# Attention maxima and scores on four tiles of 64 by 64 of the matmul array, in a transformer block kernel

## The chip, the cores and the metric

The kernel runs on one core of one Trainium2 chip, as one program. The metric is the device time of one execution in microseconds, lower is better. The core has five engines that run side by side: TensorE (PE in the profile, PEld for its weight loads), VectorE (DVE), ScalarE (ACT), GpSimd (POOL) and SyncE (SP, which here only starts DMAs). Matmul results land in PSUM, 128 partitions by eight banks of 512 fp32 values.

## The reference

One pre-norm transformer block over x of 2048 tokens by 640: sliding-window attention, then a gated feed-forward part. All inputs are fp32.

```python
S, D, H, Dh, W, F = 2048, 640, 32, 20, 256, 1536
# attention on layernorm(x): q, k, v of 32 heads with 20 features each
scores = einsum("bhqd,bhkd->bhqk", q, k) * Dh ** -0.5
mask = (iq - ik >= 0) & (iq - ik < 256)
p = softmax(where(mask, scores, -1e9))
h = x + (einsum("bhqk,bhkd->bhqd", p, v) -> (B, S, D)) @ wo
# feed-forward on layernorm(h)
h2 = h + (gelu(hn @ w_gate) * (hn @ w_up)) @ w_down
```

## The kernel before

**Blocks and windows.** The tokens are cut in 16 blocks of 128. A block of queries sees three blocks of keys: the block two before it (the oldest), the one before it, and itself (the newest); block 0 sees one and block 1 two. Of the oldest block a query in row r sees the keys in columns c > r, of the newest those with c <= r, so together the two halves of the mask make one full block.

**Numbers in two parts.** fp32 values are split into a high and a low fp16 part. For q and k the 20 features become 60 rows (high with high, high with low, low with high), so one matmul of 60 rows gives the product of one head. Heads of one parity lie on partitions 0 to 59, those of the other on 64 to 123.

**Two passes over the scores.** For each block and each unit of four heads of one parity (eight units a block) the kernel makes two passes:

- `maxima` (L1041): matmuls with queries as rows out and keys as columns (60 rows in, 128 by 128 out), into a set of three PSUM banks, one bank for each key block. `max_out` (L1135) lets VectorE copy the visible part of the oldest block over the hidden part of the newest (`copy_predicated`), then takes the maximum over the remaining two banks. When a block has all maxima, `max_rows` and `max_transpose` split them into two fp16 rows, and a DMA puts these beside the queries (rows 60 and 61).
- `scores` (L1053): the transposed product with keys as rows out and queries as columns, now with 62 rows in, so that the maximum is subtracted in the matmul. `score_out` (L1184) lets ScalarE take the exponential of all three banks, and GpSimd sets the hidden parts to zero (`affine_select`).

`value_lane` (L1198) multiplies the exponentials with the values, four heads beside each other on 32 columns of the array each, in fp32; the sums come from a column of ones.

**Two units beside each other.** There are two sets of PSUM banks (`SETS`, 0 to 2 and 3 to 5). `row_need` (L1089) picks two units of different parity, mostly one of maxima and one of scores, and `row_lane` (L1123) issues their matmuls in turn. Since one uses the lower and the other the upper 64 rows of the array, two matmuls can run at once. I call the run of matmuls of such a couple of units a stretch: 12 matmuls for each unit with three key blocks, 24 in all.

**The order of the work.** The program is written out by a planner in the kernel file itself. `Clock` and `Engine.cost` (L248) give every instruction a cost, keep a time for each engine, and the loop at the end takes the first lane of work that can start at the planned time. The order on each engine is thus fixed when the program is built, and a changed cost can change the order of all engines' instructions, and of the DMAs issued from the SP and ACT queues. The matmul part of the cost knows three layouts of the array: "full", "row" (up to 64 rows in) and "col" (up to 32 columns out); a change between them costs `SWITCH` = 0.095 us, a matmul 1/2400 us a column, at least 0.027, plus 0.0027, and one that starts beside another 0.004.

Between the stretches PE does dense work: q, k and v projections of later blocks, the output projection, and parts of the feed-forward part. After the last block (from some 560 us on) only the feed-forward part is left.

Of the kernel before, what the change touches and what calls it, by code (L numbers as in the profile page):

```python
# [23 lines left out]
P = 128  # L24
# [31 lines left out]
class Clock:  # L56
# [6 lines left out]
    def __init__(self, nc):  # L63
        self.nc = nc
        self.t = dict.fromkeys(self.NOW, 0.0)
        self.wr, self.rd, self.rings = {}, {}, {}
        self.warm, self.win, self.use = False, 0, 0.0
        self.mode, self.half = "full", 0
        self.moved, self.used = dict.fromkeys(self.NOW, 0.0), []
        self.lands = deque([0.0] * 8, maxlen=8)  # L70
        self.port = {"vector": deque(maxlen=6), "gpsimd": deque(maxlen=6)}
        for e in self.NOW:
            setattr(self, e, Engine(self, e))
# [74 lines left out]
    def warmth(self, cost, rows):  # L148

        k = int(self.t["tensor"] / self.WINDOW)  # L150
        if k > self.win:
            u = self.use / self.WINDOW if k == self.win + 1 else 0.0
            self.warm = u > 0.4 if self.warm else u > 0.75
            self.win, self.use = k, 0.0
        if not self.warm:
            cost *= 2
        self.use += cost * rows / 128
        return cost
# [19 lines left out]
    def pipe(self, at, cost):  # L178

        gaps = []  # L180
        for a, z in self.used:
            if at < a:
                gaps.append((at, min(a, at + cost)))
                cost -= gaps[-1][1] - at
                if cost <= 0:
                    break
            at = max(at, z)
        if cost > 0:
            gaps.append((at, at + cost))
        self.used = sorted(self.used[-150:] + gaps)  # L190
        return gaps[-1][1]
# [31 lines left out]
class Engine:  # L223
# [24 lines left out]
    def cost(self, op, out, ins):  # L248
        n = out.free_size()
        if op.startswith("dma_start"):  # L250
            size = n * out.partition_size() * mybir.dt.size(out.dtype)
            if op.endswith("transpose"):
                return size / 130e3
            return size / (320e3 if mybir.dt.size(out.dtype) == 4 else 150e3)
        half = mybir.dt.size(out.dtype) == 2 and ins and mybir.dt.size(ins[0].dtype) == 2
        if self.name == "tensor":
            n = ins[1].free_size()
            if op == "transpose":
                n = ins[0].partition_size()
            passes = 1 if mybir.dt.size(ins[0].dtype) == 2 else 2 if op == "transpose" else 4  # L260
            rows, cols = ins[0].partition_size(), out.partition_size()
            mode = "full" if op == "transpose" else "row" if rows <= 64 else "col"
            mode = "full" if mode == "col" and cols > 32 else mode
            k = self.clock
            switch, k.mode = SWITCH * (k.mode != mode), mode
            at = (ins[0] if mode == "row" else out).start_partition()
            beside, k.half = mode != "full" and at > k.half and not switch, at
            if beside:
                return 0.004
            return switch + k.warmth(max(n * passes / 2400, 0.027), rows) + 0.0027  # L270
        if self.name == "vector":
            m = max([n] + [i.free_size() for i in ins])
            if op in ("copy_predicated", "tensor_reduce"):
                return (0.12 if ins[-1].space == PSUM else 0.065) + 0.00106 * m
            if op == "tensor_copy" and half or op == "tensor_scalar" and m > 320:
                return (0.065 if half else 0.185) + 0.00053 * m
            return 0.065 + 0.00106 * m + 0.06 * (op == "scalar_tensor_tensor" and len(ins) == 3)
        if self.name == "scalar":
            return 0.00084 * n + (0.05 if op == "copy" or len(ins) == 1 else
                                  0.14 if ins[0].space == PSUM else 0.18)  # L280
        if self.name == "gpsimd":
            if op == "memset":
                return 0.06 + 0.0008 * n
            return 0.46 if n == 1 else 0.06 + (0.00105 if op == "affine_select" else 0.00203) * n
        raise NotImplementedError(self.name)
# [3 lines left out]
def block_kernel(ctx: ExitStack, tc: tile.TileContext, x, wqkv, wo, wg, wu, wd, out):  # L289
    nc = Clock(tc.nc)  # L290
# [9 lines left out]
    ps8 = psum.tile([P, 8 * 512], F32, name="ps8")  # L300
# [471 lines left out]
    def key(rs, pr, kb):  # L772

        return kT[rs, kb // 2 % (RK // 2), pr, kb % 2 * P:kb % 2 * P + P]
# [23 lines left out]
        pos["ones"] = 1  # L798

    nc.vector.memset(ps8[:, MM * 512:], 0.0)  # L800

    esc = const.tile([P, 1], F32, name="esc")
    hsc = const.tile([P, 1], F32, name="hsc")
# [23 lines left out]
    class Block:  # L827
        ready = wide = False
        maxima = halves = v = 0
        h, turned, normed = None, False, False  # L830
# [12 lines left out]
    at = lambda n, shape, dt, bufs=2: nc.tile(att, shape, dt, n, bufs)  # L843
# [186 lines left out]
    def window(j):  # L1030
        return list(range(max(0, j - 2), j + 1))

    def heads(u):

        return u % 2, range(4 * (u // 2), 4 * (u // 2) + 4)

    def set_view(banks):
        b = nc.box(banks[0])[1][2] // BANK
        return ps8[:, b * 512:(b + 3) * 512].rearrange("p (t c k) -> p t c k", t=3, c=4)

    def maxima(j, u, banks):  # L1041
        b = B[j]
        par, prs = heads(u)
        rs = slice(64 * par, 64 * par + 60)
        v = set_view(banks)
        ks = window(j)
        for c, pr in enumerate(prs):
            for i, kb in enumerate(ks, 3 - len(ks)):
                yield v[:, i, c, :], b.c.qT[rs, pr, b.cols], key(rs, pr, kb)
        tasks.append(max_out(j, u, banks))  # L1050
        pos["max"] += 1

    def scores(j, u, banks):  # L1053
        b = B[j]
        par, prs = heads(u)
        rs = slice(64 * par, 64 * par + 62)
        v = set_view(banks)
        ks = window(j)
        b.pt[u] = at("pt", [P, 3, 4, P], F32, 3)
        pos["units"] += 1  # L1060
        for i, kb in enumerate(ks, 3 - len(ks)):
            for c, pr in enumerate(prs):
                yield v[:, i, c, :], key(rs, pr, kb), b.c.qT[rs, pr, b.cols]
        tasks.append(score_out(j, u, banks, b.pt[u]))
        pos["score"] += 1

# [54 lines left out]
    row = []  # L1121

    def row_lane():  # L1123
        while True:
            yield ("tensor",), row_need
            gens = []
            for s, (f, x) in enumerate(row):
                (maxq if f is maxima else scoreq).remove(x)
                gens.append(f(*x, row_set(s)))
            for ops in zip_longest(*gens):  # L1130
                for op in ops:
                    if op:
                        nc.tensor.matmul(*op, start=True, stop=True)

    def max_out(j, u, banks):  # L1135
        b = B[j]
        par, prs = heads(u)
        mx = b.mx[:, 16 * par + prs[0]:16 * par + prs[0] + 4]
        n = len(window(j))
        v = set_view(banks)  # L1140
        yield on("vector", v[:, 3 - n:])
        if n == 3:
            nc.vector.copy_predicated(v[:, 2], late4, v[:, 0])
            w = v[:, 1:]
        else:
            nc.vector.tensor_tensor(v[:, 2], v[:, 2], mask4, op=ALU.add)
            w = v[:, 3 - n:]
        yield on("vector", w)
        nc.vector.tensor_reduce(mx, w.rearrange("p t c k -> p c t k"), axis=AX.XY, op=ALU.max)
        free_set(banks)  # L1150
        b.maxima += 4
        if b.maxima == H:
            tps.append(max_rows(j))
# [30 lines left out]
    def score_out(j, u, banks, pt):  # L1184
        n = len(window(j))
        v = set_view(banks)[:, 3 - n:]
        yield on("scalar", v)
        nc.scalar.activation(pt[:, 3 - n:], v, AF.Exp, scale=esc)
        free_set(banks)
        yield on("gpsimd", pt[:, 3 - n])  # L1190
        if n == 3:
            nc.gpsimd.affine_select(pt[:, 0], pt[:, 0], pattern=[[0, 4], [-1, P]],
                                    compare_op=ALU.is_ge, fill=0.0, base=-1, channel_multiplier=1)
        nc.gpsimd.affine_select(pt[:, 2], pt[:, 2], pattern=[[0, 4], [1, P]],
                                compare_op=ALU.is_ge, fill=0.0, base=0, channel_multiplier=-1)
        valq.append((j, u))
# [632 lines left out]
    rows = Lane(row_lane())  # L1829
    values = Lane(value_lane())  # L1830
    now = 0.0
# [84 lines left out]
```

## Time and profile before

| | |
|---|---|
| median of 3 runs | 997.33 us (992.41, 997.52, 997.33) |
| profiled execution, own time | 994.03 us |
| its span | 992.3 us |
| PE busy | 949.6 us, 11,637 matmuls recorded |
| weight loads (PEld) busy | 736.5 us |
| VectorE busy | 731.7 us |
| ScalarE busy | 472.7 us |
| GpSimd busy | 239.9 us |
| mean granted clock of PE | 0.998 |

The span is the time from the first to the last instruction of one profiled execution. Nearly all instructions carry the line L232, which is the helper that records every operation; the groups are told apart by the names of their tiles (`ps` is PSUM; `ps<-kT,qT` with 60 rows are maxima, `ps<-qT,kT` with 62 rows scores, `ps<-pt,vals` the value product) and by their shapes. One fp32 matmul of the program is recorded as two. A matmul's duration in the profile runs from its start to a modelled end and overlaps with its neighbours'; the time from start to start tells what it costs.

### The profile page before, as it was taken

To read this page: it belongs to the slowest core of one execution; us is meant where nothing else is said; L and a number is where in the kernel's file an instruction comes from. 1 tells how busy PE (TensorE), PEld (TensorE's weight loads), DVE (VectorE), ACT (ScalarE), POOL (GpSimd) and SP (SyncE) were. 2 spreads that over 40 slices of the span, in tenths; PEclk is the share of its full clock that TensorE was granted. 3 is DMA by queue.
4 is the path that set the end of the run, shared out by engine and by line. 5 is a ranking of instruction groups with operands and counts; after the bars stand their busy time and mean duration, and the time that the engine had idled before them with its cause. 6 is when DMAs were issued, how large, how long until landed. Compare 5 with 4: busy or idle time off the path is not lost.

```text
span 992.3 us, 27153 instructions
## 1 busy us (share of the span) xinstructions
PE 949.6 (96%) x11637; PEld 736.5 (74%) x11637; DVE 731.7 (74%) x1369; ACT 472.7 (48%) x703; POOL 239.9 (24%) x338
## 2 busy tenths in 40 slices
PE   6897999999999999999998998999999999999998
PEld 5676677777777777776764555888888888888886
DVE  6978697797856776766685689699787773994563
ACT  6624567646556555555578635553222131332120
POOL 3321234535435434334345200000111100000000
PEclk9999999999999999999999999999999999999999
DMA  9367477563453524233375523641325310120002
GB/s 351 97 167 198 121 177 187 115 155 79 99 145 58 134 69 123 69 106 78 98 181 130 156 69 112 187 120 45 94 55 148 79 68 1 45 71 14 1 2 106
DMA packets 108777, 106.89 MB, mean 108 GB/s; under 512 B 58992, under 2 KB 79728, under 8 KB 106736
## 3 DMA queue, kind: packets, MB, share of 16 engines
q1 hardware_dynamic: 85552, 94.40, 35.8%
q10 hardware_dynamic: 23104, 10.75, 4.1%
q8 instruction: 91, 1.49, 0.7%
q14 instruction: 30, 0.25, 0.1%
HBM read 71.11 MB, written 20.97 MB: 93 GB/s over the span
## 4 chain that ended last, share of the span: by engine, by line
PE 76%; DVE 10%; DMA 5%; ACT 5%; issue 2%; POOL 1%; ACTq 0%; SPq 0%; DVEq 0%; POOLq 0%
PE ps L232 76%; DVE mxs L232 2%; ACT pt L232 2%; DMA qk<-qks 1%; DVE ps L232 1%; DVE xt L232 1%; DVE qks L232 1%; DMA kT<-qk 1%; ACT wsl L232 1%; DVE kT L232 1%; POOL pt L232 1%; DMA ol<-spl 1%; DMA lxn<-h_dram 0%; ACTq L232 0%; DMA xh<-sph 0%
## 5 line engine op out<-in xcount | busy, mean ns | idle before, releaser
L232 ACT ACTIVATE pt<-ps,esc 128x1536 f32<-128x1536 f32 (+2 forms) x128 | 186.1, 1459 | 108.2 <-PE ps L232 97.9
L232 POOL TENSOR_SCALAR_AFFINE_SELECT pt<-pt 128x512 f32<-128x512 f32 x240 | 150.5, 650 | 234.9 <-ACT pt L232 232.8
L232 DVE TENSOR_REDUCE mxs<-ps 128x4 f32<-128x1024 f32 (+1 forms) x128 | 151.2, 1185 | 2.7
L232 PEld LDWEIGHTS <-kT 62*128 62x128 f16 (+1 forms) x1920 | 123.8, 95 | 27.5 <-issue 9.4
L232 DVE COPY_PREDICATED ps<-mask,ps 128x512 f32<-128x512 int32 x112 | 77.4, 693 | 77.3 <-PE ps L232 76.7
L232 DVE TENSOR_TENSOR gel<-gel,ps 128x512 f32<-128x512 f32 x140 | 93.8, 684 | 54.3 <-PE ps L232 50.1
L232 PEld LDWEIGHTS <-wu 128*128 128x128 f16 x1080 | 105.7, 98 | 12.2
L232 PEld LDWEIGHTS <-gu 128*128 128x128 f16 x888 | 86.2, 98 | 34.4 <-issue 1.3
L232 PE MATMUL ps<-kT,qT 60*128 60x128 f16 x1440 | 101.8, 218 | 7.3 <-DVE mxs L232 3.6
L232 PEld LDWEIGHTS <-qT 60*128 60x128 f16 x1440 | 79.6, 94 | 35.2 <-issue 34.5
L232 PE MATMUL ps<-qT,kT 62*128 62x128 f16 x1440 | 98.8, 218 | 3.5 <-ACT pt L232 3.3
L232 PE MATMUL ps<-pt,vals 128*21 128x128 f32 x2880 | 93.9, 276 | 6.7 <-POOL pt L232 3.2
L232 PEld LDWEIGHTS ps<-pt,vals 128*21 128x21 f32 x2880 | 73.7, 101 | 19.5 <-POOL pt L232 6.1
L232 DVE SCALAR_TENSOR_TENSOR ht<-ps,ffk,ht 128x320 f32<-128x320 f32 x96 | 51.8, 547 | 41.9 <-PE ps L232 41.7
L232 PEld LDWEIGHTS <-ah 128*128 128x128 f16 x448 | 43.7, 98 | 19.6 <-ACT ah L232 2.6
L232 ACT ACTIVATE gel<-gel,ffk 128x512 f32<-128x512 f32 x40 | 28.6, 719 | 49.9 <-DVE gel L232 49.8
L232 PE MATMUL ps<-wdh,ah 128*128 128x320 f16 x160 | 47.9, 299 | 2.2 <-ACT ah L232 2.2
L232 PE MATMUL ps<-xh,w0h 128*128 128x256 f16 x175 | 47.8, 273 | 2.1 <-ACT vals L232 1.1
L232 PE MATMUL ps<-w2l,xh 128*128 128x320 f16 x160 | 47.9, 299 | 1.5 <-DVE w2l L232 1.3
L232 PE MATMUL ps<-w3h,oh 128*128 128x320 f16 x160 | 47.9, 300 | 1.1 <-ACT oT L232 0.5
L232 PE MATMUL ps<-wdh,al 128*128 128x320 f16 x160 | 47.8, 299 | 1.2 <-DVE al L232 1.2
L232 PE MATMUL ps<-xh,w1h 128*128 128x256 f16 x175 | 47.8, 273 | 1.2 <-DVE qks L232 1.2
(252 smaller groups left out, 2267.9 us busy)
## 6 DMA issues: line engine op xcount, KB each, us to landing
wsl<-in_wd_dram SPq DMA_DIRECT2D x28, 320.0 KB
wsl<-in_wg_dram SPq DMA_DIRECT2D x33, 256.0 KB
qk<-qks ACTq DMA_DIRECT2D x64, 128.0 KB
wsl<-in_wu_dram SPq DMA_DIRECT2D x30, 256.0 KB
qT<-qk SPq DMA_DIRECT2D x16, 320.0 KB
kT<-qk SPq DMA_DIRECT2D x16, 320.0 KB
ht<-in_x_dram SPq DMA_DIRECT2D x16, 320.0 KB
h_dram<-ht SPq DMA_DIRECT2D x16, 320.0 KB
```

Source lines behind the costliest of these rows:

```text
L232: r = real(*args, **kw)
```

## The change

The array is used as four places of 64 rows by 64 columns. Each matmul of a maxima or scores unit becomes two, one for the lower and one for the upper 64 rows of the output. A unit has 24 matmuls instead of 12, and a stretch 48.

For maxima with three key blocks, `quarters` leaves out the half of the oldest block that the upper 64 queries don't see and the half of the newest that the lower 64 don't see. For each head there are then three steps of two matmuls: oldest (lower queries) with middle (upper), middle (lower) with newest (upper), and last two matmuls of 64 columns, the first half of the newest for the lower and the second half of the oldest for the upper queries. With fewer key blocks, and for scores, all is computed; the scores now go head by head as the maxima do. The tiles that VectorE, ScalarE and GpSimd then work on are the same as before. Two memsets at the start set the parts of PSUM that no maxima matmul has written to zero.

The planner gets a fourth layout, "quad", in which each of four places has a time of its own at which it is free.

```diff
@@ Engine.cost
             mode = "full" if mode == "col" and cols > 32 else mode
+            mode = "quad" if mode == "row" and cols == 64 else mode
             k = self.clock
             switch, k.mode = SWITCH * (k.mode != mode), mode
             at = (ins[0] if mode == "row" else out).start_partition()
-            beside, k.half = mode != "full" and at > k.half and not switch, at
+            if mode == "quad":
+                at = 2 * at + ins[0].start_partition()
+            if mode == "quad":
+                now = k.t["tensor"]
+                if switch or now > k.quad_end + 1e-6:
+                    k.quad, k.last = {}, now + switch - 0.004
+                k.last = max(k.last + 0.004, k.quad.get(at, 0.0))
+                k.quad[at] = k.last + max(n / 2400, 0.027) + 0.0027
+                more = max(0.001, max(k.quad.values()) - now)
+                more = switch + k.warmth(more - switch, rows)
+                k.quad_end = now + more
+                return more
+            beside, k.half = mode in ("row", "col") and at > k.half and not switch, at
@@ start
     nc.vector.memset(ps8[:, MM * 512:], 0.0)
+    for i in range(2):
+        nc.vector.memset(ps8[64:P, 3 * i * 512:3 * i * 512 + 512], 0.0)
@@ maxima
+    def quarters(n):
+        full = [((i, 0, P), (i, 0, P)) for i in range(3 - n, 3)]
+        if n < 3:
+            return full
+        return [((0, 0, P), (1, 0, P)), ((1, 0, P), (2, 0, P)), ((2, 0, 64), (0, 64, P))]
...
         for c, pr in enumerate(prs):
-            for i, kb in enumerate(ks, 3 - len(ks)):
-                yield v[:, i, c, :], b.c.qT[rs, pr, b.cols], key(rs, pr, kb)
+            for two in quarters(len(ks)):
+                for h, (i, a, z) in enumerate(two):
+                    kb = ks[i - 3]
+                    q = slice(c0 + 64 * h, c0 + 64 * h + 64)
+                    yield (v[64 * h:64 * h + 64, i, c, a:z], b.c.qT[rs, pr, q],
+                           key(rs, pr, kb)[:, a:z])
@@ scores
-        for i, kb in enumerate(ks, 3 - len(ks)):
-            for c, pr in enumerate(prs):
-                yield v[:, i, c, :], key(rs, pr, kb), b.c.qT[rs, pr, b.cols]
+        for c, pr in enumerate(prs):
+            for two in [((i, 0, P), (i, 0, P)) for i in range(3 - len(ks), 3)]:
+                for h, (i, a, z) in enumerate(two):
+                    kb = ks[i - 3]
+                    yield (v[64 * h:64 * h + 64, i, c, a:z],
+                           key(rs, pr, kb)[:, 64 * h:64 * h + 64],
+                           b.c.qT[rs, pr, c0 + a:c0 + z])
```

More of the change, by code (lines that the diff above doesn't have):

```diff
@@ L67, in __init__ @@
         self.warm, self.win, self.use = False, 0, 0.0
-        self.mode, self.half = "full", 0
+        self.mode, self.half, self.quad, self.quad_end, self.last = "full", 0, {}, 0.0, 0.0
         self.moved, self.used = dict.fromkeys(self.NOW, 0.0), []
@@ L1046, in maxima @@
         ks = window(j)
+        c0 = b.cols.start
         for c, pr in enumerate(prs):
-            for i, kb in enumerate(ks, 3 - len(ks)):
-                yield v[:, i, c, :], b.c.qT[rs, pr, b.cols], key(rs, pr, kb)
+            for two in quarters(len(ks)):
[4 more added lines that the diff above has]
+                           key(rs, pr, kb)[:, a:z])
         tasks.append(max_out(j, u, banks))
@@ L1060, in scores @@
         pos["units"] += 1
-        for i, kb in enumerate(ks, 3 - len(ks)):
-            for c, pr in enumerate(prs):
-                yield v[:, i, c, :], key(rs, pr, kb), b.c.qT[rs, pr, b.cols]
+        c0 = b.cols.start
+        for c, pr in enumerate(prs):
[5 more added lines that the diff above has]
+                           b.c.qT[rs, pr, c0 + a:c0 + z])
         tasks.append(score_out(j, u, banks, b.pt[u]))
```

## The prediction

> **What bounds the kernel now.** I read the page's busy table first, then busy time by stage, then who waits for whom, then single rows of the timeline.
>
> ```profile
> PE 949.6 (96%) x11637; PEld 736.5 (74%) x11637; DVE 731.7 (74%) x1369; ACT 472.7 (48%) x703; POOL 239.9 (24%) x338
> PE 76%; DVE 10%; DMA 5%; ACT 5%; issue 2%; POOL 1%; ACTq 0%; SPq 0%; DVEq 0%; POOLq 0%
> ```
> ```profile
> 0.00:104.00 104.00, 86.13 (x717) 69.53 (x719) 83.68 (x208) 54.44 (x108) 26.27 (x43) 1.00 0.67 201
> 104.00:560.00 456.00, 438.90 (x7434) 327.03 (x7434) 328.44 (x563) 281.38 (x368) 193.99 (x277) 1.00 0.50 121
> 560.00:992.30 432.30, 424.55 (x3502) 339.96 (x3491) 319.55 (x598) 136.84 (x228) 19.61 (x19) 1.00 0.25 71
> ```
> ```profile
> PE ps L232 <- ACT pt L232: 3.3, 6, 1.0
> PE ps L232 <- POOL pt L232: 2.4, 5, 1.7
> PE ps L232 <- ACT oT L232: 2.2, 7, 0.6
> PE ps L232 <- DVE mxs L232: 1.5, 5, 0.6
> ```
>
> TensorE (PE) is busy 96% of the span and is 76% of the chain that ended last. The stages' first number after the length is PE's busy time: attention is done between 104 and 560 us, and there PE is busy 438.9 of 456.0 us at full clock, so 17.1 us are idle. The last fence is who PE waited for in that stage (us, times, longest); these four rows are 9.4 us. VectorE, ScalarE and GpSimd have slack there. So the change counts through PE's time in the maxima and scores, and through what the planner's new order does to those waits.
>
> ```profile
> L232 PE MATMUL ps<-kT,qT 60*128 60x128 f16 x1440 | 101.8, 218 | 7.3 <-DVE mxs L232 3.6 <-DVE lyax L232 1.2 <-DMA kT<-qk 0.9
> L232 PE MATMUL ps<-qT,kT 62*128 62x128 f16 x1440 | 98.8, 218 | 3.5 <-ACT pt L232 3.3
> L232 DVE TENSOR_REDUCE mxs<-ps x128: 681/1224/1226, 59.8 to 515.4; 128x4 f32<-128x1024 f32 x120, 128x4 f32<-128x512 f32 x8
> ```
> ```profile
> 501.34 0.23 PE L232 MATMUL ps<-kT,qT 60*128 60x128 f16 x1
> 501.34 0.23 PE L232 MATMUL ps<-qT,kT 62*128 62x128 f16 x1
> 501.41 0.22 PE L232 MATMUL ps<-kT,qT 60*128 60x128 f16 x1
> 501.41 0.22 PE L232 MATMUL ps<-qT,kT 62*128 62x128 f16 x1
> 501.46 0.22 PE L232 MATMUL ps<-kT,qT 60*128 60x128 f16 x1
> 501.47 0.22 PE L232 MATMUL ps<-qT,kT 62*128 62x128 f16 x1
> ...
> 501.96 0.22 PE L232 MATMUL ps<-kT,qT 60*128 60x128 f16 x1
> 501.97 0.22 PE L232 MATMUL ps<-qT,kT 62*128 62x128 f16 x1
> 502.11 0.31 PE L232 MATMUL ps<-pt,vals 128*21 128x128 f32 x4
> ```
>
> The forms tell maxima (60 rows) from scores (62 rows): 1440 matmuls each, for 128 groups of four heads each (128 reductions), two groups to a stretch, so about 128 stretches. One whole stretch is shown: a maxima and a score matmul start together, the next pair about 56 ns later, twelve pairs in 0.63 us, and 0.14 us after the last start the next kind of matmul begins. The length in the second column (0.22 us) is latency; the start-to-start time is the cost.
>
> **The change part by part.** The sum is made against the profiled execution: span 992.3 us, own time 994.03 us.
>
> *Twice the matmuls, four at a time.* Each unit of twelve matmuls of 128 columns becomes 24 of 64 columns out: 1440 more maxima and 1440 more scores, and as many loads. A step of the new loop is lower maxima, lower score, upper maxima, upper score. Each of the four places streams 128 columns, as each of the two did, so a step should keep the 56 ns of the rows above, and twelve steps remain twelve. Of three maxima steps for a head, one streams only 64 columns; but the score matmuls beside it stream 128, and matmuls start in program order, so the next maxima matmul waits for the score ahead of it. I cost the halved step at nothing saved wherever a score runs beside it. The nearest row for four places working at once is the value product, four column places of 32:
>
> ```profile
> 502.11 1.51 PE L232 MATMUL ps<-pt,vals 128*21 128x128 f32 x48
> L232 PE MATMUL ps<-pt,vals 128*21 128x128 f32 x2880 | 93.9, 276 | 6.7 <-POOL pt L232 3.2 <-DVE qks L232 1.8 <-ACT wsl L232 1.1
> ```
> Its 48 recorded matmuls take (1.51 - 0.27) / 47 = 26 ns each, so four need 106 ns, and together they read four different fp32 streams from the same partitions; the new maxima read two fp16 streams from each partition. Reading should not bind. The bounds of a step are 28 ns (if halved ones ran free) and 106 ns (four at the row's rate); I take 56, the rows at these very shapes, because the four starts at 502.11 fall within 0.05 us of each other (below).
>
> *Weight loads.* 64 columns instead of 128:
> ```profile
> L232 PEld LDWEIGHTS <-qT 60*128 60x128 f16 x1440 | 79.6, 94 | 35.2 <-issue 34.5
> L232 PEld LDWEIGHTS <-m 128*64 128x64 f16 x16 | 1.7, 106 | 3.0 <-issue 1.5 <-DVE m L232 0.5 <-DVE ps L232 0.4
> L232 PEld LDWEIGHTS ps<-pt,vals 128*21 128x21 f32 x2880 | 73.7, 101 | 19.5 <-POOL pt L232 6.1 <-issue 4.4 <-ACT wsl L232 1.4
> L232 PEld LDWEIGHTS ps<-ident,oT 117*128 117x128 f32 x128 | 14.3, 141 | 4.5 <-ACT oT L232 2.1 <-issue 0.4
> ```
> The only 64-column fp16 load of the trace, that of the maxima's transpose, takes 106 ns against 94 for the 128-column ones. Within a stretch a load runs under the matmuls of the step before; only the first is exposed: 12 ns x 128 stretches = +1.5 us. If that cover is gone, the four loads of a step show: an estimate from 101 ns for 21 and 141 for 128 fp32 columns is 0.37 ns a column, 24 ns for 64 columns, 96 ns for four in a row.
>
> *Four starts instead of two* at the end of each stretch: the value row has four within 0.05 us, so at most about 17 ns apart; the pairs are under 10. I take 8 ns more a stretch, +1.0 us; ends 0 and 35 ns x 128 = 4.5 us.
>
> *Maxima with nothing, or a shorter score, beside them.* Blocks with shorter windows leave such tails: four rows are single in the stretch at 120.3.
> ```profile
> 120.33 0.21 PE L232 MATMUL ps<-qT,kT 62*128 62x128 f16 x1 [0.96 <-ACT pt L232]
> 120.33 0.23 PE L232 MATMUL ps<-kT,qT 60*128 60x128 f16 x1
> 120.38 0.21 PE L232 MATMUL ps<-qT,kT 62*128 62x128 f16 x1
> 120.40 0.22 PE L232 MATMUL ps<-kT,qT 60*128 60x128 f16 x1
> ...
> 120.74 0.38 PE L232 MATMUL ps<-kT,qT 60*128 60x128 f16 x4
> ```
> There a halved step saves 28 ns. Counted along the timeline: two in each of some eight such stretches, three in two more, and four in each of two stretches of maxima alone: 30 x 28 ns = -0.8 us.
>
> *Changing the array's layout*: 0.14 us from last start to next kind, of which 0.056 is streaming. No row shows a layout of 64 by 64; I count the gap unchanged, as its nearest row is the one from these very pairs to the value product's four places; a price of 0 to 30 ns more (a third of the 0.09) would be up to +4 us.
>
> *Two memsets* of 64 x 512 go behind the one of 128 x 1024 on VectorE:
> ```profile
> 1.42 0.91 DVE L232 MEMSET ps<- 128x1024 f32 x1 [0.21 <-issue]
> 2.33 0.06 DVE L232 MEMSET am<- 128x1 f32 x1
> 3.95 0.89 DVE L232 BATCH_NORM_STATS2 lstx<-xt 128x6 f32<-128x320 f32 x2 [1.57 <-DMA xt<-in_x_dram]
> ```
> At half the columns each is about 0.46 us; 0.9 us fit into the 1.57 us in which VectorE waits for x. Behind them in the queue is the layernorm, for which PE's first transposes wait; without that wait they would cost 0.9 us. I count 0.
>
> *Instructions.* PE's list grows by 5760 of 23,274.
> ```profile
> q8 instruction: 91, 1.49, 0.7%
> ```
> That is 64 B each, so +0.37 MB, some 23 fetches more beside 106 MB of other transfers: 0.
>
> *VectorE, ScalarE, GpSimd, SP*: no instruction of theirs changes beyond the memsets; the copies, reductions and exponentials still take whole tiles. No DMA is added or moved by the diff itself.
>
> *The planner.* It costed a pair at 0.0533 + 0.0027 + 0.004 = 0.060 us, twelve pairs and a switch at 0.815 us (0.867 when the upper half comes first); it now costs twelve steps at 0.095 + 12 x 0.056 + 0.012 = 0.78. What the trace shows for a stretch is 0.63 + 0.14 = 0.77. So the plan's PE clock gets 0.04 to 0.09 us a stretch earlier, nearer the chip, and many instructions of all engines, with their DMAs on the SP and ACT queues, may change places. Its worth is bounded by the 17.1 us of idle time on the one side and as much again on the other; with neither sign argued by a row I take 0.
>
> Sum: 994.0 + 1.5 + 1.0 - 0.8 = 995.7, say 996. The profiled execution is 3.3 us under the median of the three runs, 997.33, so the forecast is no change. A measurement of this kernel tells about 0.5% (5 us) from none: its three runs lie 5 us apart.
>
> **The rivals.**
>
> *Matmuls are not supplied fast enough (slower).* The densest long runs of the trace, pairs and value products, both come to 26 to 28 ns a matmul with its load. If that is a limit of supply, a stretch of 48 needs 48 x 27 = 1.30 us, not 0.68: +0.62 x 128 = 79 us, 1075. It decides from the point where fewer than 48 - 0.68 / 0.027 = 23 matmuls stand ready when a stretch begins; with 16 ready it is 16 + 32 x 27 ns = 0.86, +23 us, 1019. For it: nothing in the trace runs longer at a faster rate. Against: the four at 502.11,
> ```profile
> 502.11 0.14 PEld L232 LDWEIGHTS ps<-pt,vals 128*21 128x21 f32 x8
> ```
> with eight loads in the same 0.05 us, so twelve instructions were ready at once. Chance 0.08. The Trainium skill, "TensorE: Matmul & The Clock Gate", Part 1, puts a floor of about 25 ns on start to start, however few columns; by it the stretch would be 1.2 us and the time an estimated 1060. The trace goes against it between places of one array, with four starts in 0.05 us.
>
> *Loads of places in the same rows wait for each other (slower).* Four in a row are the 96 ns above, so a step is 96 instead of 56: 40 x 12 x 128 = +61 us, 1057; from 14 ns a load on it shows. Against: the eight loads just shown overlap and share all 128 rows; but at 21 columns (8 ns each) they don't decide it. Chance 0.06. The Trainium skill, "TensorE: Matmul & The Clock Gate", Part 3, says that a load overlaps running matmuls only where the row group differs; upper and lower half of a unit have the same rows, so by it this case would come. The value loads here run under matmuls of their own rows, which speaks against the rule for column places.
>
> *The new order waits more (slower).* A planned stretch comes earlier and finds its set of banks not yet read: 3.3 / 6 = 0.55 us a time by the ScalarE row. Eighteen more such waits in 128 stretches are +10 us, 1006. Chance 0.14.
>
> *The new order waits less (faster).* A truer PE clock lets the planner put projection work where PE waits now; eight of the 17.1 us would give 988. Chance 0.12.
>
> *The halved step counts everywhere (faster).* If maxima could run ahead of scores, four steps x 28 ns x 112 stretches = -12.5 us, 983. For it: at 120.3 the two halves run out of step, each at its own 56 ns. Against: each start still comes after the one ahead of it in the program. Chance 0.05.
>
> **How the numbers follow.** Forecast (991 to 1001): 0.55. The range 986 to 1012 holds it, most of the two cases of order and part of the -12.5 us, together about 0.8. Outside are the stretched steps, 0.14, and the tails. Faster by over 0.5% means below 992: 0.17 from two rivals and a little of the forecast's low end, 0.20. Slower: 0.06 + 0.08 + 0.14 less the mild part, 0.26. The rest, 0.54, is no change.
>
> **What would show it.** Right: stretches of 48 matmuls with about 0.63 us from first to last start, steps of 56 ns with four starts each, 0.14 us to the next kind, PE's idle time between 104 and 560 us near 17 us. Wrong: steps of 96 to 108 ns (loads or supply, told apart by whether the first steps of a stretch are quick and only the later ones slow), or a changed list of waits at an unchanged step (the order).

## The result, and the profile after

The changed kernel takes 1011.1 us, median of three runs (1004.87, 1011.1, 1011.87), against 997.33 before: ratio 1.012, 95% interval 1.0077 to 1.0164. It is slower. The forecast was no change at 996 us; the time lies at the upper end of the range, 1012. The profiled execution took 1011.1 us with a span of 1009.4 us.

The busy table and the shares of the chain that ended last, from the page of the changed kernel, then its clock row and its instruction transfers:

```profile
PE 959.1 (95%) x14517; PEld 744.7 (74%) x14517; DVE 736.0 (73%) x1371; ACT 476.9 (47%) x705; POOL 242.5 (24%) x338
PE 78%; DVE 8%; DMA 6%; ACT 4%; issue 2%; POOL 1%; ACTq 1%; SPq 0%; DVEq 0%; POOLq 0%
...
PEclk9998999999999999998999999999999999999999
...
q8 instruction: 113, 1.85, 0.8%
```

The 2880 more matmuls are there (14,517 recorded against 11,637), and only 9.5 us more of busy time. The span grew by 17.1 us. By stage (length, then busy time and count of PE, its weight loads, VectorE, ScalarE and GpSimd, granted clock, DMA share, GB/s):

```profile
0.00:104.00 104.00, 83.46 (x771) 67.43 (x771) 81.50 (x205) 53.17 (x105) 25.73 (x42) 0.97 0.63 195
104.00:560.00 456.00, 436.73 (x9750) 326.57 (x9749) 330.12 (x565) 266.37 (x355) 182.16 (x258) 0.99 0.52 121
560.00:1009.40 449.40, 438.88 (x4000) 350.68 (x3998) 324.34 (x603) 157.36 (x245) 34.62 (x39) 1.00 0.24 71
```

PE's idle time in the middle stage is 456.0 - 436.7 = 19.3 us, 2.2 us more than before; but less of the attention work is done by 560 us: its last stretch starts at 594.5 us, before at 555.5. So the stages no longer hold the same work, and the order of the whole kernel has changed. What PE waited for over the whole span (us, times, longest):

```profile
PE ps L232 <- DVE lyaxb L232: 8.4, 2, 8.0
PE ps L232 <- DVE qks L232: 7.7, 5, 4.8
PE ps L232 <- ACT pt L232: 6.0, 8, 1.9
PE ps L232 <- ACT oT L232: 5.2, 8, 1.1
PE ps L232 <- DVE mxs L232: 2.9, 7, 0.8
...
PE ps L232 <- issue: 1.0, 1, 1.0
```

Before, the same list had

```profile
PE ps L232 <- DVE qks L232: 4.5, 6, 0.9
```

One wait is long that was not there before: 4.8 us for `qks`. (The 8.0 us for `lyaxb` are at the start of the kernel, before and after.) Now the thing that was changed, a whole stretch of 48 matmuls, in the timeline of the changed kernel (start, length, form):

```profile
502.16 0.24 PE L232 MATMUL ps<-kT,qT 60*64 60x128 f16 x1
502.17 0.24 PE L232 MATMUL ps<-qT,kT 62*64 62x128 f16 x1
502.17 0.24 PE L232 MATMUL ps<-kT,qT 60*64 60x128 f16 x1
502.17 0.24 PE L232 MATMUL ps<-qT,kT 62*64 62x128 f16 x1
502.24 0.22 PE L232 MATMUL ps<-kT,qT 60*64 60x128 f16 x1
502.25 0.22 PE L232 MATMUL ps<-qT,kT 62*64 62x128 f16 x1
502.25 0.22 PE L232 MATMUL ps<-kT,qT 60*64 60x128 f16 x1
502.25 0.22 PE L232 MATMUL ps<-qT,kT 62*64 62x128 f16 x1
502.30 0.19 PE L232 MATMUL ps<-kT,qT 60*64 60x64 f16 x1
502.30 0.22 PE L232 MATMUL ps<-qT,kT 62*64 62x128 f16 x1
502.30 0.19 PE L232 MATMUL ps<-kT,qT 60*64 60x64 f16 x1
502.31 0.22 PE L232 MATMUL ps<-qT,kT 62*64 62x128 f16 x1
...
502.75 0.28 PE L232 MATMUL ps<-qT,kT 62*64 62x128 f16 x4
502.96 0.39 PE L232 MATMUL ps<-h0h,gu 128*128 128x512 f16 x1
```

Four matmuls start within 0.01 us, the next four some 56 ns later (the first step is longer). The last starts at 502.81 and the next kind 0.15 us behind it. Over all clean full stretches the length from first to last start, counted in the trace, is 648 ns after and 628 ns before.

So within a stretch the matmuls do what was forecast of them. 20 ns on some 103 such stretches are 2 us, and some 12 of the 14 us come from elsewhere. Three ways were open: the new matmuls cost something that a single stretch doesn't show; the planner's new order costs it; or the larger number of instructions does.

### The profile page after: what moved, and what is told of

It reads as the page before. It is cut to its first block, busy times and chain, and to the rows that moved or that the text cites. A ratio compares the mean times of both kernels' runs of the same rounds, so it can differ in the third digit from the quotient of the medians.

```text
span 1009.4 us, 32928 instructions
## 1 busy us (share of the span) xinstructions
PE 959.1 (95%) x14517; PEld 744.7 (74%) x14517; DVE 736.0 (73%) x1371; ACT 476.9 (47%) x705; POOL 242.5 (24%) x338
## 4 chain that ended last, share of the span: by engine, by line
PE 78%; DVE 8%; DMA 6%; ACT 4%; issue 2%; POOL 1%; ACTq 1%; SPq 0%; DVEq 0%; POOLq 0%
PE ps L232 78%; DVE mxs L232 2%; DMA xt<-in_x_dram 1%; ACT pt L232 1%; DMA qk<-qks 1%; DVE ps L232 1%; DMA ol<-spl 1%; DVE qks L232 1%; DMA wu<-in_wg_dram 1%; ACTq L232 1%; DMA wsl<-in_wg_dram 0%; DMA xh<-sph 0%; DMA xl<-spl 0%; DVE lstxb L232 0%; DMA h_dram<-ht 0%
## 5 line engine op out<-in xcount | busy, mean ns | idle before, releaser
L232 PEld LDWEIGHTS <-kT 62*64 62x64 f16 (+1 forms) x3360 | 130.0, 106 | 26.3 <-issue 8.3
L232 PE MATMUL ps<-qT,kT 62*64 62x128 f16 x2880 | 103.8, 220 | 6.2 <-ACT pt L232 6.0
L232 PEld LDWEIGHTS <-qT 60*64 60x64 f16 x2880 | 78.2, 109 | 40.0 <-issue 39.5
L232 PE MATMUL ps<-kT,qT 60*64 60x128 f16 (+1 forms) x2880 | 95.8, 213 | 6.7 <-DVE mxs L232 2.9
L232 PEld LDWEIGHTS ps<-pt,vals 128*21 128x21 f32 x2880 | 76.1, 103 | 20.4 <-issue 12.0
L232 DVE SCALAR_TENSOR_TENSOR ht<-ps,ffk,ht 128x320 f32<-128x320 f32 x96 | 51.4, 545 | 42.9 <-PE ps L232 42.7
L232 PE MATMUL ps<-w3h,ol 128*128 128x320 f16 x160 | 47.9, 299 | 1.3 <-DMA ol<-spl 1.3
```

Of the source, the lines that this page charges most:

```text
L232: r = real(*args, **kw)
```

## Experiments

**Order and matmuls apart.** The planner's choices (which lane of work next, which banks, which two units share a stretch) were written down while one kernel was built, and played back while the other was built. Then the orders of VectorE, ScalarE, GpSimd and the DMA queues are those of the first kernel (but for the two memsets), and only the matmuls are those of the second. The edit, the same in `e1`, `e2`, `e4`, `e5` and `e6`:

```diff
-        b = pick(kind)[1]
+        b = BANKS.popleft()
...
-        for lane in order:
-            if lane.alive and lane.start(now):
-                break
...
+        lane = Lane.made[LANES.popleft()]
+        if lane is rows and lane.need is row_need:
+            row[:] = [(maxima if m else scores, (j, u)) for m, j, u in ROWS.popleft()]
```

`e1`: the changed kernel's matmuls and memsets in the order of the kernel before.

> The changed matmuls (four places of 64 by 64, halves left out), but every engine's instructions and DMAs in the order of the kernel before, replayed from a list instead of planned. Theory A (the layout costs nothing, the new order cost the 14 us): stretches of 48 matmuls in 0.65 us from first to last start, PE waits and half-clock time as in the kernel before, time within 3 us of the kernel before (ratio 0.997 to 1.004). Theory B (the 64 by 64 layout itself is dear, by loads, supply or a clock that drops because the array counts as less busy): about 10 us or more above the kernel before (ratio over 1.008), with half-clock periods as in the changed kernel.

`e2`: the matmuls of before in the changed kernel's order.

> The matmuls of the kernel before (two places of 64 by 128, all of the blocks computed), but every engine's instructions and DMAs in the order of the changed kernel, replayed from a list. Theory A: it is as slow as the changed kernel, ratio to the kernel before 1.008 to 1.018, with the long waits of the changed kernel (5 us ahead of a value product near 87 us) and its half-clock periods. Theory B: back at the time of the kernel before, ratio 0.997 to 1.004.

`e3`: the changed kernel as it is, on the same chip.

> The changed kernel once more, on the chip of the other runs, for comparison. Both theories: 1005 to 1012 us, ratio to the kernel before 1.008 to 1.016.

`e4`: as `e1`, but maxima of three key blocks computed whole, so that no step is halved:

```diff
-        if n < 3:
+        if n <= 3:
             return full
```

> Four places and the order of the kernel before, but the maxima of all three key blocks computed whole, so that the halved third step is a full one. If a score matmul beside it sets the step, as predicted: stretches with three key blocks on both sides keep 0.65 us, only stretches with shorter scores go from 0.57 to about 0.63 us, and the time is within 1.5 us of the same kernel with the halves left out. If the halved step counted everywhere, it would be 12 us slower than that one.

| kernel | median us | ratio to before (95%) |
|---|---|---|
| before, same chip | 997.44 | 1 |
| e1 new matmuls, old order | 1003.6 | 1.0072 (1.0046 to 1.0097) |
| e2 old matmuls, new order | 1001.58 | 1.0059 (1.0036 to 1.0082) |
| e3 both | 1006.43 | 1.0110 (1.0082 to 1.0139) |
| e4 as e1, no halves | 1000.28 | 1.0044 (1.0016 to 1.0072) |

Neither theory holds alone. The matmuls cost 0.7% and the order 0.6%, and together they make what the change costs (0.72 + 0.59 = 1.3%, against 1.1% here and 1.2% in the first comparison). The expectations of `e1` and `e2` named two outcomes each, and both times lie between them; the 5 us wait near 87 us that `e2` was to show isn't in its trace. The halves are worth nothing that these times can tell: `e4` is no slower than `e1`, its median is 3.3 us lower where 1.5 us either way were expected, and the intervals overlap. Counted in the traces, a full stretch is 648 ns with halves and 648 without; only stretches with fewer scores beside the 24 maxima gain, 572 against 645 ns with 16 scores.

The longer stretch explains 20 ns x 103 = 2.1 us less 0.4 for the tails, some 1.7 us, of the 6 us of `e1`. Most of the rest stands in its list of waits, in a row that the kernel before hasn't got at all:

```profile
PE ps L239 <- issue: 3.1, 3, 2.4
```

"Issue" means that nothing in the profile made PE wait. The timeline of `e1` at the longest one:

```profile
448.20 0.22 PE L239 MATMUL ps<-kT,qT 60*64 60x128 f16 x1
448.21 0.22 PE L239 MATMUL ps<-qT,kT 62*64 62x128 f16 x1
450.82 0.24 PE L239 MATMUL ps<-qT,kT 62*64 62x128 f16 x1 [2.40 <-issue]
450.82 0.24 PE L239 MATMUL ps<-kT,qT 60*64 60x128 f16 x1
```

PE stops in the middle of a stretch, and the matmul that it stops at has no semaphore to wait for. What came in between is in the DMA view of the window from 448.25 to 450.80 us of the same kernel (queue, packets, MB, share):

```profile
q1 hardware_dynamic: 105, 0.23, 25.2%
q8 instruction: 1, 0.02, 2.8%
```

One packet of instructions. PE's instructions come in packets of 256: 23,274 of them in 91 packets before, 29,034 in 113 after. In the trace this packet starts 0.08 us after PE's last start, takes 1.13 us, and PE goes on 1.41 us after its end: 2.6 us from start to start. Every wait for "issue" in the kernels of this document falls on the same place in a group of 256 instructions (the 168th to the 178th of the recorded ones), and all but two of these 57 waits end 1.2 to 1.7 us after a packet's end. Counted that way, over 0.3 us from start to start, `e1` has three (4.0 us), `e4` two (2.6 us), the changed kernel one (1.2 us), `e3`, `e2` and the kernel before none. A packet takes some 1.05 us, but can start as late as 4.6 us after PE has passed the place before: 4.6 + 1.1 + 1.4 are the 7.1 us in which PE got from place to place here, and its own work was 4.5 of them. From place to place the kernel before never needs less than some 6.2 us; the kernels with four places take 3.5 us where maxima stretches lie close together.

**Is it the number of instructions?** `e5` doubles the maxima and score matmuls with their loads without the new layout: those of before, each cut in two of 64 streamed columns, in the order of before. `e6` doubles them again in four places.

```diff
-                for op in ops:
-                    if op:
-                        nc.tensor.matmul(*op, start=True, stop=True)
+                for n in (slice(0, 64), slice(64, P)):
+                    for op in ops:
+                        if op:
+                            o, w, m = op
+                            nc.tensor.matmul(o[:, n], w, m[:, n], start=True, stop=True)
```

> The kernel before, in its own order, with its two places of 64 by 128, but each maxima and score matmul split into two of 64 streamed columns with a load each: as many PE instructions as in the changed kernel, the same columns streamed, nothing of the 64 by 64 layout. Theory S (PE runs short of instructions now and then): stalls of 0.5 to 2.5 us without any semaphore wait, as in the two kernels with the new matmuls in the old order, and 1.5 to 5 us over the kernel before. Theory L (the layout of 64 by 64 makes the cost): no such stall, within 1.5 us of the kernel before.

`e6` is `e1` with the same edit and, as in `e4`, no halves:

> Four places, whole blocks, order of the kernel before, and each of these matmuls split into two of 64 streamed columns: 96 matmuls a stretch, the same columns streamed. Theory S: the stalls without a wait become many, and the time is 15 us or more over the kernel before. Theory L: the steps may be up to 2 ns longer by the loads, 24 x 2 x 128 = 6 us, and no stall without a wait; 1000 to 1008 us.

Measured: `e5` 1010.46 us, ratio 1.0135 (1.0098 to 1.0172); `e6` 1077.36 us, ratio 1.0822 (1.0775 to 1.0868); the kernel before 995.66 us on that chip. Two rows of the waits of `e5`, then the first of `e6` and its instruction transfers:

```profile
PE ps L239 <- DVE qks L239: 8.6, 6, 3.9
...
PE ps L239 <- issue: 2.5, 1, 2.5
```
```profile
PE ps L239 <- issue: 38.1, 43, 5.3
```
```profile
q8 instruction: 158, 2.59, 1.0%
```

`e5` stalls at the same place of a group of 256 without the four places, twice, 3.2 us; so these stalls go with the number of instructions and not with the layout. In `e6` PE needs as little as some 2 us for 256 instructions, and stalls 47 times, 50 us as counted from start to start. Its stretches take 813 ns instead of the 628 of the kernel before, with 23 ns less to the next kind: 105 x 162 ns = 17 us more. That is 67 of the 82 us; its mean clock is 0.983 against 0.995 of the kernel before on that chip, some 11 us by the rate worked out below. The 14.8 us of `e5` are only partly supply: 3.2 us of stalls, 105 x 30 ns = 3.2 us of longer stretches (684 ns, with 26 ns less to the next kind), some 4 us more of waits for `qks` than before, and a lower clock (0.9915 against 0.995, some 3 us). The expectation of 1.5 to 5 us had left out the last two.

A dense run of instructions is not the whole condition. `e12` below has the matmuls of the kernel before, and its list of waits has

```profile
PE ps L232 <- issue: 0.6, 1, 0.6
```

It stands at the same place of a group (the 174th), where the packet started late, 4.3 us after PE had passed the place before. So the order of before can be short of instructions too; it happened once there, for 0.8 us from start to start.

**How much is an order worth?** `e2` showed 0.6% for one other order. `e7`, `e8` and `e12` take the kernel before and change one cost in the planner by 0.001 or 0.0005 us, nothing else:

```diff
-SWITCH = 0.095
+SWITCH = 0.096
```

> The kernel before with only the planner's cost of a change of layout at 0.096 instead of 0.095 us; no instruction is another, only their order. If the order in the kernel before is one picked among many and any new one costs some us: 1 to 10 us slower. If the changed kernel's order was a particularly bad one: within 2 us of the kernel before.

`e8`: 0.094.

> The same with 0.094 us: another order of the same instructions. Picked order: 1 to 10 us slower than the kernel before. Otherwise within 2 us.

`e9` and `e10` do the same in the changed kernel (0.096 and 0.094):

> The changed kernel with only the planner's cost of a change of layout at 0.096 instead of 0.095 us: the same new matmuls in another order. If the order is a draw: between 4 and 25 us slower than the kernel before (the layout's own 4 to 5 us, plus a draw of 0 to 20). If the changed kernel's order was an unlucky one that a small step undoes: at the 4 to 6 us of the new matmuls in the old order.

> The same with 0.094 us. Order as a draw: 4 to 25 us slower than the kernel before.

`e11` keeps the matmuls of before and gives the planner the change's rule for their cost, with two places:

```diff
+            if mode == "row":
+                now = k.t["tensor"]
...
+                k.last = max(k.last + 0.004, k.quad.get(at, 0.0))
+                k.quad[at] = k.last + max(n / 2400, 0.027) + 0.0027
...
-            beside, k.half = mode != "full" and at > k.half and not switch, at
+            beside, k.half = mode == "col" and at > k.half and not switch, at
```

> The matmuls of the kernel before, but the planner costs a pair of them by the change's own rule (each half of the array free again when its matmul is through), so that a planned stretch is 0.78 us instead of 0.815 to 0.867, as the trace has it. The prediction's rival that a truer clock lets PE wait less: faster than the kernel before by 3 us or more. Order as a draw: 0 to 20 us slower.

`e12`: the kernel before with `SWITCH` 0.0955.

> The kernel before with the planner's cost of a change of layout at 0.0955 us: an order that differs from it in few places (some 110 of 17,000 rows on PE, 8 on SP). If few places make few differences: within 2 us of the kernel before.

| order | matmuls | median us | ratio to before (95%) |
|---|---|---|---|
| e11 truer cost of a stretch | old | 990.63 | 0.9938 (0.9916 to 0.9959) |
| e12 0.0955 | old | 991.77 | 0.9960 (0.9935 to 0.9984) |
| e8 0.094 | old | 999.32 | 1.0032 (1.0012 to 1.0053) |
| e2 the changed kernel's | old | 1001.58 | 1.0059 (1.0036 to 1.0082) |
| e7 0.096 | old | 1019.42 | 1.0230 (1.0203 to 1.0258) |
| e1 that of before | new | 1003.6 | 1.0072 (1.0046 to 1.0097) |
| e9 0.096 | new | 1006.17 | 1.0098 (1.0062 to 1.0133) |
| e3 the changed kernel's | new | 1006.43 | 1.0110 (1.0082 to 1.0139) |
| e10 0.094 | new | 1018.84 | 1.0227 (1.0195 to 1.0259) |

With the same matmuls the orders span 2.9%, and those of `e7`, `e8` and `e12` come from one cost moved by some 1% or less. (`e7`, `e8` were timed beside a kernel before of 995.66 us, `e9` to `e12` beside one of 996.53.) There is no direction in it: 0.0955 gains, 0.096 loses most, 0.094 loses a little. Two expectations had the size wrong: `e7` loses 24 us where 1 to 10 were expected, and `e12`, expected within 2 us, gains 5. The middle stage of `e7`, then of `e11`, each with its largest wait for a tile of attention (over the whole span):

```profile
104.00:560.00 456.00, 427.02 (x7069) 319.65 (x7070) 323.53 (x546) 262.18 (x347) 181.06 (x257) 0.98 0.47 116
```
```profile
PE ps L232 <- ACT pt L232: 9.3, 10, 1.9
```
```profile
104.00:560.00 456.00, 442.14 (x7255) 327.38 (x7255) 335.75 (x586) 274.42 (x364) 188.89 (x265) 1.00 0.50 121
```
```profile
PE ps L232 <- ACT pt L232: 3.9, 7, 1.0
```

The bad order leaves PE idle for 29.0 us of this stage and runs it at a lower clock; the good one for 13.9 us at full clock. `e11` beats both kernels, by 6 us and by some 16 us, as the rival of a truer clock had it; that the truer cost is the reason isn't shown, since `e12` comes near it with no truer one.

**Why a wait costs more than its length.** In the changed kernel PE's 4.8 us wait for `qks` ends at 91.9 us. The stretches before and behind (the clock stands third from the end):

```profile
86.00:92.00 6.00, 1.16 (x33) 0.84 (x34) 1.35 (x3) 1.54 (x3) 0.30 (x1) 0.86 0.46 147
92.00:97.00 5.00, 5.00 (x55) 3.37 (x55) 2.40 (x3) 1.56 (x4) 0.34 (x1) 0.50 0.44 117
```

PE runs at half clock for 5 us after it, though it has work throughout. The chain that ended last, behind that wait:

```profile
80.87 9.48 DMA qk<-qks
...
91.09 0.70 DVE qks L232
...
91.92 6.13 PE ps L232 x58
```

By this chain a store of `qks` that took 9.48 us (7.61 before) held its buffer. The new order alone doesn't bring this wait: `e3` is the same kernel in another execution, and its row is

```profile
PE ps L232 <- DVE qks L232: 3.1, 5, 0.8
```

while `e5`, in the order of before, has one of 3.9 us. The changed kernel's profiled execution has six such periods of half clock, of 3.4 us or twice that, each after a wait or during one; the kernel before has one:

```profile
451.20:454.60 3.40, 3.40 (x68) 2.71 (x56) 1.62 (x2) 1.73 (x2) 1.22 (x2) 0.50 0.51 154
```

It needs no long wait: this period follows two of 0.8 and 0.7 us within 2 us. Over 131 runs of all these kernels, within a kernel the time falls by 0.89 us (standard error 0.09) for each 0.001 of mean clock: so part of the spread of one kernel's runs goes with such periods.

## Why the prediction was wrong, step by step

**The stretch: right.** Forecast +12 ns for the first load and +8 ns for four starts; measured +20 ns together, 648 against 628. The first step takes 80 ns instead of 66, and the four starts of a step span 10 ns where the two spanned 4. The other steps kept their 56 ns, the way to the next kind its 148 ns. There were some 103 whole stretches rather than 128, so +2.1 us where the sum had 2.5. The two memsets took 1.02 us and went into VectorE's wait for x, as counted. The groups by form show the price of a 64-column load, 109 ns where 106 were taken:

```profile
L232 PEld LDWEIGHTS <-qT 60*64 60x64 f16 x2880 | 78.2, 109 | 40.0 <-issue 39.5
L232 PE MATMUL ps<-kT,qT 60*64 60x64 f16 x896 | 71.1, 190 | 0.0
```

**Halved steps: right.** The 896 halved matmuls above save nothing beside a score (648 ns with them and without) and 53 ns in stretches with 16 scores instead of 24 beside the maxima (625 before, 572 after; forecast 2 x 28 = 56). The rival that had them count everywhere is out.

**Loads of places in the same rows: right, they don't wait.** The step would have been 96 ns and is 56. The Trainium skill, "TensorE: Matmul & The Clock Gate", Part 3, lets a load overlap only matmuls of another row group; the four places here share row groups two by two, and this trace doesn't agree.

**Supply at 27 ns a matmul: the rival is out as a rate, but there is a supply limit.** The 48 starts of a stretch lie within 0.648 us, 13.8 ns from one to the next. The floor of 25 ns that the Trainium skill, "TensorE: Matmul & The Clock Gate", Part 1, puts on start to start doesn't hold between places of one array here.

**The planner's order at 0: this step failed.** No row argued for a sign, but that made the price unknown and not 0, and the bound of 17 us was too narrow as well: one order is 24 us worse than that of before. For the order that the change happens to make, the price is +0.59% (`e2`), 4 to 6 us, about half of the result. "The new order waits more" was given 0.14. That the price is paid in PE's waits, as this rival has it, isn't shown for this order: the profiled execution of `e2`, 997.33 us, is the fastest of its nine, and PE idles in it for 43.8 us (span less busy) against 42.7 before.

**"Instructions: 0": this step failed too.** It weighed 23 packets against 106 MB of traffic, and so asked about bandwidth. What counts is the time to the next packet: PE runs dry when it works off 256 instructions faster than the next come, 3.5 us at the shortest against a delay of up to 4.6 us, 1.05 us of transfer and 1.4 us until use. In the profiled executions of the kernels with these matmuls it cost 0 to 4.7 us (`e10`), and 50 us in `e6`. The rival of supply looked for it at the wrong length, within a stretch instead of over several. In the changed kernel itself the two traces have 1.2 us and none (`e3`), so there it is a small part of what was missed.

**Not in the sum: the clock.** The forecast had no term for a lower clock behind a wait. In the profiled execution of after the clock stood at half for 23.8 us, 22.3 of them busy, which can cost up to 11.2 us of work; before it was 3.4 us, up to 1.7.

How this adds up can be read off the busy tables. For `e3`, whose span is 1002.0 us, the table begins

```profile
PE 955.6 (95%) x14517; PEld 742.4 (74%) x14517; DVE 736.6 (74%) x1371; ACT 476.8 (48%) x705; POOL 242.6 (24%) x338
```

| against before | span | PE idle | PE busy | half clock, at most | longer stretches |
|---|---|---|---|---|---|
| changed kernel, 1011.1 us | +17.1 | +7.6 | +9.5 | 9.5 | 1.7 |
| the same, `e3`, 1003.72 us | +9.7 | +3.7 | +6.0 | 4.7 | 1.7 |

The last two columns are parts of the busy time, and make it up within 2 us. Of the 7.6 us, 4.8 are the wait for `qks` that `e3` hasn't got: so some of the difference between these two executions isn't the change. In the medians of one chip the change costs 9 us (`e3` against before); the matmuls alone cost 3 to 6 us (`e4`, `e1`) and the order alone 4 (`e2`), each with what the clock lost in those runs. What makes an instruction packet start late, so that a given kernel stalls in one place and not in another, stays open; so does which waits make the order's price, and why a given wait turns into half clock.

## What to carry to other kernels

Cutting matmuls into more places saves nothing while a neighbour that starts in order streams the full width, and it doubles their instructions: compare the shortest time in which an engine works off one packet of instructions with the time of the next packet, and read a PE wait put down to "issue" in the middle of a run of matmuls as that. In a kernel whose order is planned from costs, play the old order back before blaming or praising an edit, and build a few orders with a cost moved by 1%: their spread (here -0.4% to +2.3%) is what a change has to beat. A wait, even one under 1 us with another close to it, may cost PE as much again in half clock behind it. One profiled execution can hold a wait that the next execution of the same kernel hasn't got: profile a kernel twice before putting a wait down to the change.

## What the runs showed of the chip that was not expected

- PE's instructions arrive by DMA in packets of 256 (16 KB) while the kernel runs; a packet takes 0.9 to 2.3 us, and PE goes on 1.2 to 1.7 us after its end where it had run dry. Stalls of up to 5.5 us (`e6`).
- Matmuls of four places, 64 by 64, each with a load of its own, start 13.8 ns apart on average, and the loads of 109 ns hide under steps of 56 ns.
- After waits of 4.8 us (the changed kernel) and of 0.8 and 0.7 us (before) PE ran at half clock for 3.4 us or more while busy; the mean clock of the orders ranges from 0.986 (`e7`) to 0.9985 (`e11`), which at 0.89 us for 0.001 is 11 of the 29 us between these two.
